# A decode attention kernel: maximum and bias moved ahead of the next keys' turns, a new order of the last loads

## The chip, the cores and the metric

The kernel runs on one core of a Trainium2 chip. The metric is the device time of one execution in microseconds (us); several executions give a median. A core has five engines that run their own instruction queues in order: TensorE (PE, matrix products), VectorE (DVE), ScalarE (ACT), GpSimd (POOL) and SyncE (SP, which here only issues loads). They wait for each other through semaphores. Sixteen DMA engines move data from the chip's memory into the core's.

## The reference

One decode step of grouped-query attention beside a token-mixing MLP, all in float32. With B = 8, D = 512, 32 query heads, 8 key/value heads, 8192 cached positions and head size 128:

```python
xn = layernorm(x)
q = xn @ wq                                   # 32 heads of 128
scores = einsum("bhqd,bhkd->bhqk", q, k) * 128 ** -0.5   # each key head serves 4 query heads
o = einsum("bhqk,bhkd->bhqd", softmax(scores), v)
out = x + o @ wo + mixer(xn)                  # mixer: layernorm, outer product with w1, + b1, gelu, product with w2
```

The key and value caches are 8 x 8 blocks of 8192 x 128 floats each: 64 blocks of keys and 64 of values, 4 MB a block, each read once.

## The kernel before, in words

The 64 pairs of a key/value head and a batch row are worked through one after the other; block i has head h = i // 8 and batch row b = i % 8. Everything is scheduled by hand: each engine executes its instructions in the order in which the program writes them, and semaphores are put in for the data and the buffers.

**Loads.** A ring of five 4 MB buffers (`raw`) holds keys and values. `load_next` (L68) takes the next entry of the list `order` and issues it on SP; each entry has a place number, 2i for the keys and 2i + 2.5 for the values of block i, and the list is sorted by it. In the kernel before, the last keys have number 124.2 (L55), so that they come right after the keys of block 62. A buffer comes free when qk (for keys) or pv (for values) has read it; `load_next` is called at the end of both. When the list is empty, the next call loads the last two heads' output weights (`wo`) into the buffer after that, as eight loads (L85). The first keys and the last values come in pieces.

**A slot.** `slot(i)` (L380) does the scores of block i, the values product of block i - 1, and prepares the keys of block i + 1:

- `qk(i)` (L222): 32 matmuls on PE from the turned keys into the scores S (tile `s`, L228).
- `turn(i, a)` (L215): DVE transposes a quarter of the keys in place, in 32 x 32 blocks (L218). qk needs all four quarters.
- `sm_max(i)` (L236): DVE takes the row maximum of S (tile `mr`, L238). `sm_bias(i)` (L241): a matmul on PE spreads the maxima (L243) and a DVE instruction takes the minimum over the head's rows as bias `nb` (L246).
- `sm_exp(i)` (L249): ACT computes exp with that bias (L252). `sm_place(i)` (L257): a permuting matmul on PE (L259) and a DVE transpose into `pt` (L261).
- `pv(i)` (L267): 32 matmuls on PE from `pt` and the values (tile `o`, L272).
- `o_pick(i)` (L281): three DVE instructions pick and add the parts that count (L283, L286, L287). `o_place(i)` (L290): a matmul puts them into the head's output (tile `mh`, L294).

After these come, in some slots, the mixer's steps on ACT and POOL, the copies of the next head's queries (`q_place`, DVE), and at a head's first slot the sums, the scaling and `o_project` for the head before (L311 to L328).

**The end.** The last two blocks are written out (L418 to L444): the order of their turns, of pv(61), pv(62) and of the picks is given there by hand; then pv(63) in four pieces as its values land, `o_last`, the scaling, one `o_project` for two heads (L320), and the output's store.

Of the kernel before, what the change touches and what calls it, by code (L numbers as in the profile page):

```python
# [14 lines left out]
B, D, HQ, HKV, SK, DH, F = 8, 512, 32, 8, 8192, 128, 1792  # L15
REP = HQ // HKV
P = 128
NT = SK // P
# [9 lines left out]
N_IT = B * HKV  # L28
# [5 lines left out]
def attn_mixer_kernel(ctx: ExitStack, tc: tile.TileContext, x, kc, vc, wq, wo, w1, b1, w2, b2, out):  # L34
# [12 lines left out]
    def misc():  # L47
        return ps_m.tile([P, 512], F32, name="misc")
# [3 lines left out]
    KR, VR = {}, {}  # L52
    order = []
    for i in range(N_IT):
        order.append((2 * min(i, N_IT - 1.9), kc, KR, i))  # L55
        order.append((2 * i + 2.5, vc, VR, i))
    order.sort(key=lambda o: o[0])
    order.reverse()
# [9 lines left out]
    def load_next():  # L68
        if order:
            _, src, to, i = order.pop()  # L70
            h, b = divmod(i, B)
            t = ring.tile([P, NT, DH], F32, name="raw")
            rows = src[b, h].rearrange("(p t) d -> p t d", p=P)
            at = 0
            for n in (NT // 4,) * 4 if to is KR and i == 0 else (NT // 2, NT // 4, NT // 8, NT // 8) if not order else (NT,):
                nc.sync.dma_start(t[:, at:at + n, :], rows[:, at:at + n, :])
                at += n
            to[i] = t
        elif HKV - 1 not in wos:
            t = ring.tile([P, NT, DH], F32, name="raw")  # L80
            t = t.rearrange("p (h r c) d -> p h r (c d)", h=4, r=REP)
            for h in (HKV - 2, HKV - 1):
                rows = wo[h * REP * DH:(h + 1) * REP * DH, :].rearrange("(r p) n -> p r n", p=P)
                wos[h] = t[:, h % 2]
                for r in range(REP):  # L85
                    nc.sync.dma_start(wos[h][:, r, :], rows[:, r, :])

    wos = {}
# [15 lines left out]
    for _ in range(RING - 2):  # L104
        load_next()
# [109 lines left out]
    def turn(i, a, w=NT // 4):  # L215
        if i < N_IT:
            t = KR[i][:, a:a + w, :].rearrange("p t d -> p (t d)")
            nc.vector.transpose(t, t)  # L218
# [3 lines left out]
    def qk(i):  # L222
        h, b = divmod(i, B)
        S[i] = ps_s.tile([P, 512], F32, name="s")
        kt = KR.pop(i).rearrange("p (u g) d -> p g u d", g=NG)
        for j in range(NB):
            for g in range(NG):
                nc.tensor.matmul(S[i][g * Q:(g + 1) * Q, :], W[h % 2][:, b, j, :], kt[:, g, :, j * Q:(j + 1) * Q],  # L228
                                 start=(j == 0), stop=(j == NB - 1))
        load_next()  # L230
# [5 lines left out]
    def sm_max(i):  # L236
        mr = work.tile([P, 1], F32, name="mr")
        nc.vector.tensor_reduce(mr, S[i], AX.X, ALU.max)  # L238
        st[i] = mr

    def sm_bias(i):  # L241
        m = misc()
        nc.tensor.matmul(m[:, :P], st[i].to_broadcast([P, P]), ident, start=True, stop=True)  # L243
        t = one.tile([P, P], F32, name="sq")
        nb = work.tile([P, 1], F32, name="nb")
        nc.vector.tensor_tensor_reduce(t, m[:, :P], hmask, -SCALE, 3.0e38, ALU.add, ALU.min, nb)  # L246
        st[i] = nb

    def sm_exp(i):  # L249
        h, b = divmod(i, B)  # L250
        p = t2k.tile([P, 512], F32, name="t2k")
        nc.scalar.activation(p, S.pop(i), AF.Exp, bias=st[i], scale=SCALE, accum_out=LR[h % 2][:, b:b + 1])  # L252
        st[i] = p
# [3 lines left out]
    def sm_place(i):  # L257
        m = misc()
        nc.tensor.matmul(m, perm, st.pop(i), start=True, stop=True)  # L259
        PT[i] = work.tile([P, 512], F32, name="pt")  # L260
        nc.vector.transpose(PT[i], m)  # L261
# [5 lines left out]
    def pv(i, u0=0, u1=NU):  # L267
        if u0 == 0:
            O[i] = ps_o.tile([P, 512], F32, name="o")
        for u in range(u0, u1):  # L270
            c = u % NB
            nc.tensor.matmul(O[i][c * Q:(c + 1) * Q, :], PT[i][:, u * Q:(u + 1) * Q],  # L272
                             VR[i][:, u * NG:(u + 1) * NG, :].rearrange("p t d -> p (t d)"),
                             start=(u < NB), stop=(u >= NU - NB))
        if u1 == NU:
            del VR[i], PT[i]
            load_next()
# [3 lines left out]
    def o_pick(i):  # L281
        om = t2k.tile([P, 512], F32, name="t2k")
        nc.vector.tensor_tensor(om.rearrange("p (g d) -> p g d", g=NG), O.pop(i).rearrange("p (g d) -> p g d", g=NG),  # L283
                                dm.unsqueeze(2).to_broadcast([P, NG, DH]), ALU.mult)
        ob = work.tile([P, 256], F32, name="ob")
        nc.vector.tensor_add(ob, om[:, :256], om[:, 256:])  # L286
        nc.vector.tensor_add(ob[:, :DH], ob[:, :DH], ob[:, DH:])  # L287
        OB[i] = ob

    def o_place(i):  # L290
        h, b = divmod(i, B)
        if b == 0:
            MH[h] = ps_h.tile([P, 512], F32, name="mh")
        nc.tensor.matmul(MH[h][:, b * REP:(b + 1) * REP], OB.pop(i)[:, :DH], sel, start=True, stop=True)  # L294
# [13 lines left out]
    def o_sums(h):  # L308
        m = misc()
        for r in range(REP):  # L310
            nc.tensor.matmul(m[:, r * B:(r + 1) * B], sel[:, r:r + 1].to_broadcast([P, P]), LR[h % 2], start=True, stop=True)  # L311
        RD[h] = work.tile([P, REP, B], F32, name="rd")
        nc.vector.reciprocal(RD[h], m[:, :REP * B].rearrange("p (r b) -> p r b", r=REP))

    def o_scale(h):
        nc.vector.tensor_tensor(OTS[h % 2].rearrange("p r (b s) -> p r b s", s=BS)[:, :, :, 0],
                                MH.pop(h)[:, :REP * B].rearrange("p (b r) -> p r b", r=REP), RD.pop(h), ALU.mult)

    def o_project(*hs):
        m = misc()  # L320
        n = 0
        for h in hs:
            for r in range(REP):
                n += 1
                for j in range(NB):
                    nc.tensor.matmul(m[j * Q:(j + 1) * Q, :D // NB], OTS[h % 2][:, r, :], wos[h][:, r, quarter[j]],  # L326
                                     start=(n == 1), stop=(n == REP * len(hs)))
        nc.vector.tensor_add(yacc, m[:, :D // NB], yacc)  # L328
# [5 lines left out]
    def mx_begin(b):  # L334
        m = misc()
        nc.tensor.matmul(m, ident[:B, b:b + 1].to_broadcast([B, P]), hn, start=True, stop=True)  # L336
        hb = one.tile([P, D], F32, name="hb")
        nc.scalar.copy(hb, m)
        acc = one.tile([P, D], F32, name="macc")
        nc.gpsimd.memset(acc, 0.0)  # L340
        mx[b] = (hb, acc)

    def mx_step(b, j):
        hb, acc = mx[b]
        g = one.tile([P, D], F32, name="g")
        nc.scalar.activation(g, hb, AF.Gelu_apprx_tanh, bias=b1t[:, j:j + 1], scale=w1t[:, j:j + 1])  # L346
        nc.gpsimd.tensor_scalar(g, g, w2t[:, j:j + 1], 1.0, op0=ALU.mult, op1=ALU.mult)  # L347
        nc.gpsimd.tensor_add(acc, acc, g)  # L348
# [25 lines left out]
    quart = NT // 4  # L374
# [3 lines left out]
    LAST = N_IT - 1  # L378

    def slot(i):  # L380

        h, b = divmod(i, B)
        qk(i)
        turn(i + 1, 0)
        sm_max(i)
        turn(i + 1, quart)
        if i:
            pv(i - 1)
        turn(i + 1, 2 * quart)
        sm_bias(i)  # L390
        if i:
            o_pick(i - 1)
            o_place(i - 1)
        sm_exp(i)
        turn(i + 1, 3 * quart)
        sm_place(i)
        if b == 0:
            mx_begin(h)
            if h:
                o_sums(h - 1)  # L400
                o_scale(h - 1)
                if h + 1 < HKV:
                    o_project(h - 1)
        k = 2 if h + 1 < HKV else 3
        for j in range(k * b, min(k * b + k, NF)):
            mx_step(h, j)
        if b == 2 and h + 2 < HKV:
            load_wo(h)
        if 3 <= b < 3 + NB and h + 1 < HKV:
            q_place(h + 1, b - 3)  # L410
        if b == (B - 1 if h + 1 < HKV else B - 3):
            mx_end(h)
# [3 lines left out]
    for i in range(LAST - 1):  # L416
        slot(i)
    h = HKV - 1  # L418
    qk(LAST - 1)
    turn(LAST, 0)  # L420
    sm_max(LAST - 1)
    turn(LAST, quart)
    sm_bias(LAST - 1)
    sm_exp(LAST - 1)
    turn(LAST, 2 * quart)
    sm_place(LAST - 1)
    turn(LAST, 3 * quart)
    qk(LAST)
    sm_max(LAST)
    sm_bias(LAST)  # L430
    sm_exp(LAST)
    pv(LAST - 2)
    o_pick(LAST - 2)
    o_place(LAST - 2)
    sm_place(LAST)
    pv(LAST - 1)
    o_pick(LAST - 1)
    o_place(LAST - 1)
    o_sums(h)
# [33 lines left out]
```

## Time and profile before

| | |
|---|---|
| median of 3 runs | 1304.92 us (1304.08 to 1305.86) |
| the profiled execution's own time | 1303.8 us |
| its span, first to last instruction | 1301.9 us |
| busy: PE, DVE, ACT, POOL | 791.1, 805.8, 289.4, 231.0 us |
| mean granted clock of TensorE | 0.765 |
| read from memory | 553.69 MB, 425 GB/s over the span |

How to read it: times are of one profiled execution. A row of the groups gives line, engine, operation, output<-inputs, shapes and count, then busy time and the mean of one in ns, then the engine's idle time just before these instructions and what ended most of it. A row in order of time gives start, duration, and for a part of the rows the idle time before in brackets. The chain of waits is followed back from the last instruction and shown in order of time: start, duration, and what it was. A row of a stretch gives its bounds and length, the busy time of PE, of PE's weight loads, of DVE, ACT and POOL with counts, then the granted clock of TensorE, the share of the DMA engines, and GB/s.

### The profile page before, as it was taken

The numbers are of one execution on the slowest core, as the hardware profiler recorded it, in microseconds if no ns is written. First come the engines' busy times: TensorE is split into PE (matmuls) and PEld (weight loads), VectorE is DVE, ScalarE is ACT, GpSimd is POOL, SyncE is SP. The second block draws the span as 40 slices with busy tenths as digits, with TensorE's granted clock in tenths as the row PEclk, the third lists the DMA queues.
The fourth block names the chain that finished last, engine by engine and source line by source line (L and its number), as shares of the span: only waits on it lengthen the run. The fifth ranks groups of instructions, "written<-read, shape, count | busy, mean of one in ns | idle before, by whom it ended". The sixth has DMA issues, their size and how long they took to land.

```text
span 1301.9 us, 12448 instructions
## 1 busy us (share of the span) xinstructions
PE 791.1 (61%) x5178; PEld 260.6 (20%) x5178; DVE 805.8 (62%) x834; ACT 289.4 (22%) x365; POOL 231.0 (18%) x244
## 2 busy tenths in 40 slices
PE   3375657755566646656558556575465775576466
PEld 2121112111121112211113111121112211122112
DVE  2676575575665665665765756755666657656662
ACT  0032221221222321212202213023121223213210
POOL 1022211212112211212112112022120222113210
PEclk9688777777778678687687786777776777767778
DMA  9999999999999999999999999999999999999995
GB/s 403 434 434 428 429 434 431 434 432 431 431 432 435 430 434 433 431 430 430 434 431 433 433 432 428 434 433 431 430 432 433 432 435 432 435 432 430 429 432 216
DMA packets 24139, 554.50 MB, mean 426 GB/s; under 512 B 2540, under 2 KB 2572, under 8 KB 6932
## 3 DMA queue, kind: packets, MB, share of 16 engines
q1 hardware_dynamic: 23940, 553.67, 98.9%
q8 instruction: 41, 0.67, 0.2%
q14 instruction: 14, 0.11, 0.0%
q0 software_dynamic: 128, 0.02, 0.0%
q10 hardware_dynamic: 16, 0.02, 0.0%
HBM read 553.69 MB, written 0.02 MB: 425 GB/s over the span
## 4 chain that ended last, share of the span: by engine, by line
DMA 58%; PE 22%; DVE 13%; issue 4%; ACT 3%; SPq 0%; ACTq 0%; DVEq 0%
DMA raw<-in_A_k_cache_dram 56%; DVE raw L218 10%; PE s L228 10%; PE o L272 6%; PE misc L259 3%; ACT L252 2%; DMA raw<-in_A_wq_dram 2%; DVE mr L238 1%; ACT t2k L252 1%; PE s L188 1%; PE misc L336 1%; PE misc L326 1%; PE misc L311 0%; DVE t2k L283 0%; DVE sq L246 0%
## 5 line engine op out<-in xcount | busy, mean ns | idle before, releaser
L218 DVE STREAM_TRANSPOSE raw<-raw 128x2048 f32<-128x2048 f32 x256 | 582.1, 2294 | 347.8 <-DMA raw<-in_A_k_cache_dram 347.8
L228 PE MATMUL s<-raw,w 128*32 128x512 f32 x2048 | 324.3, 790 | 20.3 <-issue 11.8
L347 POOL TENSOR_SCALAR g<-g,w2t 128x512 f32<-128x512 f32 x112 | 77.7, 693 | 897.5 <-ACT g L346 897.5
L272 PE MATMUL o<-raw,pt 128*32 128x512 f32 x2048 | 231.0, 592 | 0.0
L294 PE MATMUL mh<-sel,ob 128*128 128x4 f32 x126 | 35.0, 348 | 314.6 <-DVE ob L287 314.6
L252 ACT ACT_TABLE_LOAD x55 | 70.6, 1283 | 590.4 <-DVE nb L246 590.3
L348 POOL TENSOR_TENSOR macc<-macc,g 128x512 f32<-128x512 f32 x112 | 144.4, 1289 | 9.4
L259 PE MATMUL misc<-t2k,perm 128*128 128x512 f32 x128 | 125.0, 1077 | 17.2 <-ACT t2k L252 17.2
L228 PEld LDWEIGHTS s<-raw,w 128*32 128x32 f32 x2048 | 77.5, 144 | 279.5 <-issue 260.0
L346 ACT ACTIVATE g<-hb,b1t,w1t 128x512 f32<-128x512 f32 x112 | 91.0, 813 | 128.8 <-POOL macc L348 128.1
L243 PE MATMUL misc<-ident,mr 128*128 128x128 f32 x128 | 32.3, 336 | 127.7 <-DVE mr L238 127.7
L294 PEld LDWEIGHTS mh<-sel,ob 128*128 128x128 f32 x126 | 29.5, 290 | 328.6 <-DVE ob L287 328.6
L272 PEld LDWEIGHTS o<-raw,pt 128*32 128x32 f32 x2048 | 62.4, 110 | 156.9 <-issue 156.8
L252 ACT ACTIVATE t2k<-s,nb 128x512 f32<-128x512 f32 x64 | 44.0, 687 | 197.8 <-DVE nb L246 197.2
L261 DVE STREAM_TRANSPOSE pt<-misc 128x512 f32<-128x512 f32 x64 | 45.6, 712 | 39.1 <-PE misc L259 39.0
L346 ACT ACT_TABLE_LOAD x54 | 69.3, 1283 | 1.4
L238 DVE TENSOR_REDUCE mr<-s 128x1 f32<-128x512 f32 x64 | 42.2, 659 | 24.3 <-PE s L228 24.2
L243 PEld LDWEIGHTS misc<-ident,mr 128*128 128x128 f32 x128 | 19.6, 193 | 185.2 <-DVE mr L238 177.7
L283 DVE TENSOR_TENSOR t2k<-o,dm 128x512 f32<-128x512 f32 x63 | 43.2, 685 | 6.1 <-PE o L272 6.1
L211 DVE COPY w<-qt 32x128 f32<-32x128 f32 x64 | 37.0, 616 | 0.7
L259 PEld LDWEIGHTS misc<-t2k,perm 128*128 128x128 f32 x128 | 30.7, 297 | 21.6 <-ACT t2k L252 21.6
L286 DVE TENSOR_TENSOR ob<-t2k 128x256 f32<-128x256 f32 x63 | 26.8, 425 | 2.2
(75 smaller groups left out, 198.2 us busy)
## 6 DMA issues: line engine op xcount, KB each, us to landing
raw<-in_A_k_cache_dram SPq DMA_DIRECT2D x63, 4096.0 KB, 38.2
raw<-in_A_v_cache_dram SPq DMA_DIRECT2D x63, 4096.0 KB, 32.0
raw<-in_A_wq_dram SPq DMA_DIRECT2D x2, 4096.0 KB, 17.1
wo<-in_A_wo_dram SPq DMA_DIRECT2D x6, 1024.0 KB, 39.5
raw<-in_A_k_cache_dram SPq DMA_DIRECT2D x4, 1024.0 KB, 26.9
raw<-in_A_v_cache_dram SPq DMA_DIRECT2D x1, 2048.0 KB, 32.6
raw<-in_A_wo_dram SPq DMA_DIRECT2D x8, 256.0 KB, 7.3
raw<-in_A_v_cache_dram SPq DMA_DIRECT2D x1, 1024.0 KB, 34.7
```

What stands on the lines that cost most here:

```text
L218: nc.vector.transpose(t, t)
L228: nc.tensor.matmul(S[i][g * Q:(g + 1) * Q, :], W[h % 2][:, b, j, :], kt[:, g, :, j * Q:(j + 1) * Q], start=(j == 0), stop=(j == NB - 1))
L238: nc.vector.tensor_reduce(mr, S[i], AX.X, ALU.max)
L243: nc.tensor.matmul(m[:, :P], st[i].to_broadcast([P, P]), ident, start=True, stop=True)
L252: nc.scalar.activation(p, S.pop(i), AF.Exp, bias=st[i], scale=SCALE, accum_out=LR[h % 2][:, b:b + 1])
L259: nc.tensor.matmul(m, perm, st.pop(i), start=True, stop=True)
L261: nc.vector.transpose(PT[i], m)
L272: nc.tensor.matmul(O[i][c * Q:(c + 1) * Q, :], PT[i][:, u * Q:(u + 1) * Q], VR[i][:, u * NG:(u + 1) * NG, :].rearrange("p t d -> p (t d)") ...
L294: nc.tensor.matmul(MH[h][:, b * REP:(b + 1) * REP], OB.pop(i)[:, :DH], sel, start=True, stop=True)
L346: nc.scalar.activation(g, hb, AF.Gelu_apprx_tanh, bias=b1t[:, j:j + 1], scale=w1t[:, j:j + 1])
L347: nc.gpsimd.tensor_scalar(g, g, w2t[:, j:j + 1], 1.0, op0=ALU.mult, op1=ALU.mult)
L348: nc.gpsimd.tensor_add(acc, acc, g)
```

## The change

In `slot`, the maximum and the bias of block i come directly after qk(i), ahead of the first turn of the next keys; pv, pick and output placement of block i - 1 follow that first turn; then exp, the second turn, the placement of the probabilities, and the last two turns. The written-out end gets a similar order: pv(61) moves ahead of the placement of block 62, its pick behind qk(63), and pv(62) ahead of the placement of block 63. The last keys keep their regular number in the list of loads (after the values of block 61) and come in four pieces. The end weights come as one load for head 6 and two (three rows, one row) for head 7.

```diff
@@ the list of loads, load_next
-        order.append((2 * min(i, N_IT - 1.9), kc, KR, i))
+        order.append((2 * i, kc, KR, i))
...
-            for n in (NT // 4,) * 4 if to is KR and i == 0 else (NT // 2, NT // 4, NT // 8, NT // 8) if not order else (NT,):
+            for n in (NT // 4,) * 4 if to is KR and i in (0, N_IT - 1) else (NT // 2, NT // 4, NT // 8, NT // 8) if not order else (NT,):
...
-                for r in range(REP):
+                for r in (slice(0, REP),) if h < HKV - 1 else (slice(0, REP - 1), slice(REP - 1, REP)):
                     nc.sync.dma_start(wos[h][:, r, :], rows[:, r, :])
@@ slot
         qk(i)
+        sm_max(i)
+        sm_bias(i)
         turn(i + 1, 0)
-        sm_max(i)
-        turn(i + 1, quart)
         if i:
             pv(i - 1)
-        turn(i + 1, 2 * quart)
-        sm_bias(i)
-        if i:
             o_pick(i - 1)
             o_place(i - 1)
         sm_exp(i)
-        turn(i + 1, 3 * quart)
+        turn(i + 1, quart)
         sm_place(i)
+        for a in (2, 3):
+            turn(i + 1, a * quart)
@@ the end
     qk(LAST - 1)
     turn(LAST, 0)
     sm_max(LAST - 1)
-    turn(LAST, quart)
     sm_bias(LAST - 1)
     sm_exp(LAST - 1)
-    turn(LAST, 2 * quart)
+    turn(LAST, quart)
+    pv(LAST - 2)
     sm_place(LAST - 1)
-    turn(LAST, 3 * quart)
+    for a in (2, 3):
+        turn(LAST, a * quart)
     qk(LAST)
+    o_pick(LAST - 2)
+    o_place(LAST - 2)
     sm_max(LAST)
     sm_bias(LAST)
     sm_exp(LAST)
-    pv(LAST - 2)
-    o_pick(LAST - 2)
-    o_place(LAST - 2)
+    pv(LAST - 1)
     sm_place(LAST)
-    pv(LAST - 1)
     o_pick(LAST - 1)
     o_place(LAST - 1)
     o_sums(h)
```

## The prediction

> **What bounds the kernel now.** I read the page first, then one middle slot in order of time, then the chain of waits at both ends, then a table of two-microsecond stretches for the clock.
>
> ```profile
> span 1301.9 us, 12448 instructions
> PE 791.1 (61%) x5178; PEld 260.6 (20%) x5178; DVE 805.8 (62%) x834; ACT 289.4 (22%) x365; POOL 231.0 (18%) x244
> DMA  9999999999999999999999999999999999999995
> L218 DVE STREAM_TRANSPOSE raw<-raw 128x2048 f32<-128x2048 f32 x256 | 582.1, 2294 | 347.8 <-DMA raw<-in_A_k_cache_dram 347.8
> L228 PE MATMUL s<-raw,w 128*32 128x512 f32 x2048 | 324.3, 790 | 20.3 <-issue 11.8
> raw<-in_A_k_cache_dram SPq DMA_DIRECT2D x63, 4096.0 KB, 38.2
> raw<-in_A_v_cache_dram SPq DMA_DIRECT2D x63, 4096.0 KB, 32.0
> ```
>
> The DMA engines are busy in every slice but the last, and VectorE (DVE) stands idle for 347.8 us, all of it ahead of a turn and for keys that have not landed. So loading sets the pace. The lead of the loads is large: a key load is issued 38.2 us before it lands. 324.3 us over 64 blocks is 5.07 us for one qk.
>
> ```profile
> 657.24 2.31 DVE L218 STREAM_TRANSPOSE raw<-raw 128x2048 f32<-128x2048 f32 x1 [5.31 <-DMA raw<-in_A_k_cache_dram]
> 659.47 0.65 DVE L238 TENSOR_REDUCE mr<-s 128x1 f32<-128x512 f32 x1
> 660.05 4.48 DVE L218 STREAM_TRANSPOSE raw<-raw 128x2048 f32<-128x2048 f32 x2
> 664.45 0.25 DVE L246 CUSTOM_DVE_ANT_0 sq<-misc,hmask 128x128 f32<-128x128 f32 x1
> 666.03 2.30 DVE L218 STREAM_TRANSPOSE raw<-raw 128x2048 f32<-128x2048 f32 x1
> 666.92 2.08 PE L259 MATMUL misc<-t2k,perm 128*128 128x512 f32 x2 [0.17 <-ACT t2k L252]
> 669.04 0.72 DVE L261 STREAM_TRANSPOSE pt<-misc 128x512 f32<-128x512 f32 x1 [0.71 <-PE misc L259]
> 669.36 4.87 PE L228 MATMUL s<-raw,w 128*32 128x512 f32 x32
> 676.42 2.31 DVE L218 STREAM_TRANSPOSE raw<-raw 128x2048 f32<-128x2048 f32 x1 [6.48 <-DMA raw<-in_A_k_cache_dram]
> ...
> 691.70 0.36 DVE L313 RECIPROCAL rd<-misc 128x32 f32<-128x32 f32 x1 [3.09 <-PE misc L311]
> 692.40 1.94 PE L326 MATMUL misc<-wo,ot 128*32 128x128 f32 x32 [0.74 <-PE misc L311]
> ```
>
> In this slot the four turns start when the keys land at 657.24. Maximum, bias and the sums of the block before (pick) lie between the turns, on the same engine. What matters: while DVE turns, TensorE (PE) computes the values product pv of the block before, and nothing on DVE has to wait for it. Two turns from 660.05 to 664.45 cost 2.2 us each. The slot is done at 674.23, 2.2 us before the next keys land at 676.42.
>
> ```profile
> 49.19 6.08 PE s L228 x32
> ...
> 66.87 5.76 PE s L228 x32
> ...
> 121.23 2.31 DVE raw L218
> ...
> 1246.04 2.31 DVE raw L218
> ...
> 1258.39 3.84 PE s L228 x32
> ...
> 1266.23 2.09 PE misc L259 x2
> ...
> 1271.30 6.02 PE s L228 x32
> ...
> 1277.35 0.70 DVE mr L238
> ...
> 1278.10 0.49 PE misc L243 x2
> 1278.58 3.61 PE o L272 x32
> ...
> 1282.29 0.70 DVE t2k L283
> ...
> 1283.02 0.44 DVE ob L286
> ...
> 1283.48 0.30 DVE ob L287
> ...
> 1283.82 0.39 PE mh L294 x2
> 1284.21 0.96 PE misc L259 x2
> ...
> 1290.73 0.90 PE misc L311 x8
> 1291.63 3.61 PE o L272 x32
> ...
> 1296.87 1.93 PE misc L326 x64
> ```
>
> These are the chain of waits at the start (to 121.23) and at the end. The turns at 121.23 and 1246.04 are the first turns of blocks 5 and 62, each begun as its keys landed: 1124.81 us for 57 blocks, so **loading takes 19.73 us a block** (the six loads of output weights in it).
>
> **The slot's order.** No operation is added or removed in a slot; the order on DVE and PE changes, so the price is that of the waits. Before, turn(i+1, 0) needs only its keys. After, it stands behind the maximum and bias of block i, which need qk(i); and pick(i-1) stands in front of the second turn, with pv(i-1) only just issued behind the bias matmul. Queued behind that wait are three turns, the transpose of the probabilities, and then qk(i+1) on PE. The slot becomes a loop in which DVE and PE take turns. Its length from the end of qk, step by step: maximum from 1277.35, bias matmul to 1278.58, pv to 1282.20 (with pv, not the turn of 2.2 us beside it, ending last: 3.61), pick to 1283.78. With the qk before ending at 1277.32 that is 6.46. Then the second turn 2.2, the transpose 0.72 and two turns 4.4: in all 13.8 us, plus qk itself. Placement matmuls (0.39 and 0.96) fit under the second turn; exp on ScalarE is ready before them.
>
> **What qk then takes.** Rows give 3.84 (at 1258.39) to 6.08 (at 49.19). The clock is the reason:
>
> ```profile
> 1240.00:1242.00 2.00, 2.00 (x16) 0.59 (x12) 0.00 (x0) 0.81 (x1) 1.06 (x2) 0.52 1.14 492
> 1252.00:1254.00 2.00, 0.00 (x0) 0.00 (x0) 2.00 (x4) 0.39 (x1) 0.00 (x0) 0.54 0.95 410
> 1258.00:1260.00 2.00, 2.00 (x24) 0.71 (x20) 2.00 (x3) 0.00 (x0) 0.00 (x0) 0.75 0.99 426
> 1274.00:1276.00 2.00, 2.00 (x16) 0.44 (x12) 0.00 (x0) 0.00 (x0) 0.00 (x0) 0.50 0.97 408
> ```
>
> The number after the five engines is the granted clock. It falls while PE idles (0.54 from 1252) and comes back only some time into work (0.75 from 1258, in the qk of 3.84, which followed other matmuls directly). The qk of 6.02 at 1271.30 came 3.0 us after the placement matmul had ended at 1268.32 and ran at 0.50 up to 1276. In the new order the placement ends some 3 us after pv, and qk starts 9 us after pv: about 6 us without a matmul in front of every qk. The nearest rows are therefore 6.02 and 6.08, and I take 6.02. The loop is 19.8 us, just over the 19.73 that loading needs: **the compute becomes the bound**, and the wait of 347.8 us for keys disappears.
>
> The Trainium skill, page "TensorE: Matmul & The Clock Gate", section "Why this matters for your kernels", speaks against the new order too: it wants no PE gaps over about 3 us between bursts, since one idle window sends the clock back to half. By its Part 1 a qk that starts cold runs at half rate for one to two windows of 3.4 us, an estimate from that page of 5.3 to 7.0 us for qk and 19.1 to 20.8 for the loop; the rows above agree as far as they go (6.02, 6.08).
>
> **The sum.** qk(0) stays at 49.19. The first slot has no pv, and its sum in the new order (6.08, maximum and bias 1.3, bias minimum 0.4, four turns 8.8, transpose 0.72) is 17.3 against the 17.68 of the rows, so qk(1) stays at 66.9. From there 61 loops of 19.8 make 1207.8. In six slots a head ends: reciprocal, scaling and o_project, from 691.70 to 694.34 in the rows, come between the last turn and qk, 2.6 us, of which the 1.94 of matmuls give back half by raising the clock earlier: 1.6 each, 9.8 in all. qk(62) starts at 1284.5.
>
> **The end.** From the end of qk(62) at 1290.5: maximum and bias 1.27, pv(61) 3.61, placement 1.0, transpose 0.72, two turns 4.5, so qk(63) starts 11.1 later and ends at 1307.6. Then maximum and bias 1.27, pv(62) 3.61, placement 0.96, transpose 0.77, pick 1.49, its placement 0.43, the sums 0.90 (row 1290.73), the last pv 3.61, and the 6.66 from its end at 1295.24 to the end of the span: 19.7, where it was 24.6. This is the change's gain, 4.9 us, since pv(61) no longer stands behind qk(63). Against it stands qk(63) ending at 1307.6 in place of 1277.3. The end is 1327.3.
>
> **The loads.** The last keys follow V61 instead of leading it, in four pieces, and the end weights come as three loads, not eight.
>
> ```profile
> SPq L86 <- DMA raw<-in_A_v_cache_dram: 20.0, 6, 9.3
> 1288.00:1290.00 2.00, 0.74 (x8) 0.00 (x0) 1.12 (x3) 0.00 (x0) 0.00 (x0) 1.00 0.37 142
> ```
>
> SP waited 20.0 us in issuing the eight for earlier loads to land, and the last bytes came before 1290, while o_project starts at 1296.87: hidden before, hidden after. Three issues more for keys and five fewer for weights cost nothing as long as each load is issued well ahead. Between the slots the queue keeps the same order, and a load issued at the end of qk or pv has 38.2 or 32.0 us of lead. The cover goes only where loading is the bound: then V61 (half of 19.73 after K62 at 1246.04) and a quarter of the keys put the first piece at about 1258.3, the last at 1265.8, against turns that would start at about 1257 and 1271 (below): at most 1 us, beside qk(62). I take nothing, bounds 0 and 1.
>
> **The rivals.** *Loading stays the bound.* If qk keeps its mean of 5.07 us, the loop is 18.9, under 19.73, and the middle takes as long as now. For it: the mean is the mean of all 64 blocks in this kernel. Against it: there the placement matmul ran straight into qk (666.9 to 669.4 in the middle slot), and the new order puts three DVE operations between the two. Its time: K62 lands at 1246.04, four turns, pick and transpose take 11.1 (8.8, 1.49, 0.72 and the hand-overs), qk(62) starts at 1257.2 and ends at 1262.2; 11.1, 5.07 and 19.7 later the span ends at 1298.1. That is 3.8 less than now, 1301 by the median. With 6.02 for the two last blocks alone it is 1300.0, or 1303. It decides this way when 13.8 plus qk plus 0.16 (9.8 over 61) is under 19.73, so at a qk below 5.8 us.
>
> *The loop locks to the clock's steps.* The rows of the clock put its changes at 1241.92 (0.04 of a stretch of two at full clock), 1252.16 and 1259.0: 10.24 and 6.84 apart, three and two times 3.41. A qk at full clock all through is about 3.6 us (pv's 3.61 is the same 32 matmuls at 1.00), and each us at half clock adds half a us. A loop a little under 20.48, six steps, starts each qk a little earlier in its step, so that the full clock comes later and the loop grows; one over 20.48 shrinks. It would settle at 20.48, with the head's extra work swallowed by the same rule: qk(62) starts at 66.9 + 61 x 20.48 = 1316.2, takes 6.7, then 11.1, 6.7 and 19.7: 1360.4, by the median 1363. For it: the two long rows of qk (6.02, 6.08) come within 0.7 us of the 6.7 that this takes. Against it: a step that is mostly filled with qk might already bring the clock back, and then a loop near 18.8 comes in between and the mean falls to about 19.8. The Trainium skill's page named above states the ground for it in Part 1, a free-running window of 3413 ns; the steps of 3.41 in the trace agree.
>
> *The change does nothing in the middle*, because DVE's idle time covers what is added: that is the first rival seen from DVE, whose work stays 805.8 us in all. It fails because the loop counts PE's qk and pv as well.
>
> **How the numbers follow.** The sum goes by one profiled execution of 1303.8 us, 1.9 over its span; the median of the runs is 1.1 above it. 1327.3 + 1.9 + 1.1 = 1330. Chances: compute bound without locking 0.65 (1310 to 1347: 0.3 us of loop either way, times 61), locked 0.20 (1347 to 1364), loading stays the bound 0.12 (1299 to 1304), others 0.03. For 8 in 10 the range leaves out about 0.1 at each end: 1303 to 1360. Measured from no change, a difference of 0.2% (2.6 us) is about what this kernel's runs can tell. Faster by more takes the first rival with a short qk at the end: 0.08. Within 0.2%: 0.05. Slower: 0.87.
>
> **What would show it.** Right: the wait of DVE for keys (347.8 us) falls to a few tens; new waits, about 1.4 us a slot of pick for pv (3.61 less the turn of 2.2) and about 6 us a slot of qk for the last turn; the mean of qk goes from 5.07 to about 6 us; first turns come 19.8 to 20.5 us apart within a head; SP waits longer for free slots and the DMA share falls a little. From the end of qk(63) to the end of the span 19.7, not 24.6. Wrong: DVE still waiting 2 us a slot for keys, or qk with a mean under 5.8. The weakest step is the 6.02: 0.2 us on it are 12 us of the end.

## The result and the profile after

The changed kernel takes 1334.91 us (median of 4 runs, 1333.40 to 1336.38) against 1304.70 before (4 runs too): a ratio of 1.023, 95% interval 1.0213 to 1.0248. It is slower by 30.2 us; 1330 was predicted. The profiled execution has a span of 1334.5 us where that of before had 1301.9.

The page of the changed kernel: span, DMA in 40 slices, three groups (busy and mean, then the idle time before them and what ended it), and the lead of the loads in the last column.

```profile
span 1334.5 us, 12442 instructions
DMA  9999999999999999999999999999999999999991
L228 PE MATMUL s<-raw,w 128*32 128x512 f32 x2048 | 382.3, 915 | 337.1 <-issue 286.3
L218 DVE STREAM_TRANSPOSE raw<-raw 128x2048 f32<-128x2048 f32 x256 | 579.8, 2284 | 0.3 <-issue 0.2
L283 DVE TENSOR_TENSOR t2k<-o,dm 128x512 f32<-128x512 f32 x63 | 43.5, 690 | 58.4 <-PE o L272 58.4
raw<-in_A_v_cache_dram SPq DMA_DIRECT2D x63, 4096.0 KB, 15.4
raw<-in_A_k_cache_dram SPq DMA_DIRECT2D x62, 4096.0 KB, 20.2
```

The wait of the turns for keys, 347.8 us before, is 0.3 us of idle time in all. In its place pick waits 58.4 us for pv, qk sits idle before its first matmul for 337.1 us, and one qk takes 382.3 / 64 = 5.97 us, not 5.07. A key load is issued 20.2 us ahead of its landing, not 38.2: fewer loads are under way ahead of their use, and SP's waits for free buffers add up to 1194 us, not 1162. The DMA slices hardly show it; a 9 means 90% or more, and 98.9% of the engines' span on that queue has only become 97.4%.

One slot in the middle, in the chain of waits (start, duration, what):

```profile
629.87 6.64 PE s L228 x32
636.51 0.02 issue
636.53 0.70 DVE mr L238
637.24 0.04 issue
637.28 0.49 PE misc L243 x2
637.77 3.62 PE o L272 x32
641.38 0.02 issue
641.41 0.70 DVE t2k L283
...
643.35 0.98 PE misc L259 x2
644.33 5.89 issue
650.22 5.01 PE s L228 x32
...
668.93 5.89 PE s L228 x32
```

No DMA stands in it. From the end of qk to the next qk it is 13.7 us both times (636.51 to 650.22, 655.23 to 668.93), and qk itself varies: 6.64, 5.01, 5.89. The 5.89 us of "issue" are time in which DVE ends the second turn, transposes the probabilities and does the last two turns, and PE has nothing to do.

### The profile page after: what moved, and what is told of

Read it like the earlier page. It is cut to its first block, busy times and chain, and to the rows that moved or that the text cites. A ratio compares the mean times of both kernels' runs of the same rounds, so it can differ in the third digit from the quotient of the medians.

```text
span 1334.5 us, 12442 instructions
## 1 busy us (share of the span) xinstructions
PE 786.0 (59%) x5178; PEld 249.1 (19%) x5178; DVE 796.0 (60%) x834; ACT 289.4 (22%) x365; POOL 232.3 (17%) x244
## 3 DMA queue, kind: packets, MB, share of 16 engines
q1 hardware_dynamic: 24292, 553.67, 97.4%
## 4 chain that ended last, share of the span: by engine, by line
PE 57%; issue 23%; DVE 16%; DMA 2%; ACT 1%; SPq 0%; ACTq 0%; DVEq 0%
PE s L228 29%; PE o L272 17%; DVE raw L218 5%; PE misc L259 4%; DVE mr L238 3%; DVE t2k L283 3%; DVE ob L286 3%; PE misc L243 2%; DMA raw<-in_A_wq_dram 2%; PE mh L294 2%; DVE ob L287 1%; PE misc L326 1%; PE s L188 1%; ACT L346 1%; DVE pt L261 1%
## 5 line engine op out<-in xcount | busy, mean ns | idle before, releaser
L228 PE MATMUL s<-raw,w 128*32 128x512 f32 x2048 | 382.3, 915 | 337.1 <-issue 286.3
L347 POOL TENSOR_SCALAR g<-g,w2t 128x512 f32<-128x512 f32 x112 | 81.3, 726 | 908.8 <-ACT g L346 908.8
L272 PE MATMUL o<-raw,pt 128*32 128x512 f32 x2048 | 234.3, 598 | 0.0
L228 PEld LDWEIGHTS s<-raw,w 128*32 128x32 f32 x2048 | 95.1, 160 | 605.7 <-issue 545.5
L294 PE MATMUL mh<-sel,ob 128*128 128x4 f32 x126 | 24.3, 263 | 108.5 <-DVE ob L287 108.5
L283 DVE TENSOR_TENSOR t2k<-o,dm 128x512 f32<-128x512 f32 x63 | 43.5, 690 | 58.4 <-PE o L272 58.4
L259 PE MATMUL misc<-t2k,perm 128*128 128x512 f32 x128 | 72.8, 651 | 2.5 <-ACT t2k L252 2.5
L294 PEld LDWEIGHTS mh<-sel,ob 128*128 128x128 f32 x126 | 18.7, 188 | 165.6 <-DVE ob L287 164.8
L246 DVE CUSTOM_DVE_ANT_0 sq<-misc,hmask 128x128 f32<-128x128 f32 x64 | 18.6, 291 | 44.1 <-PE misc L243 44.1
L286 DVE TENSOR_TENSOR ob<-t2k 128x256 f32<-128x256 f32 x63 | 34.6, 549 | 2.1
L340 POOL MEMSET macc<- 128x512 f32 x8 | 4.2, 524 | 117.5 <-PE misc L353 117.5
## 6 DMA issues: line engine op xcount, KB each, us to landing
raw<-in_A_k_cache_dram SPq DMA_DIRECT2D x62, 4096.0 KB, 20.2
raw<-in_A_v_cache_dram SPq DMA_DIRECT2D x1, 1024.0 KB, 18.7
raw<-in_A_v_cache_dram SPq DMA_DIRECT2D x2, 512.0 KB, 20.2
```

## The experiments

The theory on record: the slot has become a loop of DVE and PE of 13.7 us plus a qk that starts at half clock, longer than the 19.73 us of loading. The rivals: the new loads cost the time; the loop is long by its waits and the clock only goes along; and, about the size, that the loop locks to the clock's steps.

### Which part

The new slot alone (old loads, old end), and everything but the new slot:

```diff
# e1_slot_only: the kernel before, with the slot of the change
# e2_end_loads: the changed kernel, with the slot of before
```

> The kernel before with the new order inside the slot alone; loads, end weights and the written-out end as before. Loop theory (the slot has become a loop through VectorE and TensorE of about 13.7 us plus a qk of about 6 us, longer than the 19.73 us that loading needs): 1335 to 1342 us, the whole loss, and some us more since the old end is kept; VectorE's wait for keys near 0. Rival (the new order of the loads, the keys in pieces or the three weight loads cost the time): about 1305 us.

> The changed kernel with the old order inside the slot; new loads, weights and end kept. Loop theory: loading is the bound again, 1300 to 1305 us, VectorE's wait for keys near 340 us. Rival (the loads cost the time): about 1335 us.

Measured: the slot alone 1337.64 us, ratio 1.0254 (1.0239 to 1.0269); without it 1304.62, ratio 0.9997 (0.9988 to 1.0007), with 350.9 us of DVE waiting for keys. The whole loss is the slot's. Two more runs take what is left apart:

```diff
# e10_loads_only: the kernel before, with the new order, pieces and weight loads
# e11_end_only: the kernel before, with the new written-out end
```

> The kernel before with the new loads alone (last keys in their regular place and in four pieces, three weight loads); slot and end as before. No theory gives them a price: 1304 to 1306 us.

> The kernel before with the new written-out end alone. The prediction's gain of 4.9 us behind qk(63) if the last pv stayed at 3.61 us: 1300 us. With the last pv at half clock as in e2_end_loads (6.43 us): 1303 to 1305 us.

Measured: 1305.07, ratio 1.0004 (0.9994 to 1.0013), and 1305.43, ratio 1.0008 (0.9998 to 1.0017). Neither is worth anything by itself, and the gain that the prediction gave to the end is missing in e2_end_loads and in e11_end_only (last pv 6.43 and 5.99 us). With the new slot the two together are worth 2.7 us: e1_slot_only, which lacks them, takes 1337.64 us and the changed kernel 1334.91.

### Is the clock a cause

Matmuls that nothing reads are added to the changed kernel, in PE's gap of the slot:

```diff
+    def warm(n):
+        m = misc()
+        for _ in range(n):
+            for g in range(NB):
+                nc.tensor.matmul(m[g * Q:(g + 1) * Q, :], bsel[:, :Q], rj.rearrange("p j i d -> p (j i d)"), start=True, stop=True)
...
         sm_place(i)
+        warm(12)        # e3_warm;  warm(6) in e5_warm_half
         for a in (2, 3):
             turn(i + 1, a * quart)
```

> The changed kernel with 48 matmuls per slot that nothing reads, set on TensorE between the placement of the probabilities and the next qk (5.2 us at full clock), while VectorE does the last two turns. No wait is removed and work is added. Loop theory with the clock as its last term: qk starts at full clock and takes 3.6 to 4.2 us, not 5.97; the loop is 17.3 to 17.9 us, under 19.73, so that loading is the bound again: 1299 to 1306 us. Rival (the loop is long by its waits and the clock only goes along with it): 1335 us or more.

Measured: 1508.86 us, ratio 1.1558 (1.1537 to 1.1579). The size was wrong: 48 such calls are 96 matmul instructions and take twice what was planned. In order of time:

```profile
675.03 10.51 PE L384 MATMUL misc<-rj,bsel 128*32 128x512 f32 x96
685.35 3.62 PE L228 MATMUL s<-raw,w 128*32 128x512 f32 x32
```

qk now waits for them, but it takes 3.62 us. So the time could not decide between the theories, and half as many were tried:

> The kernel of e3_warm with half the matmuls that nothing reads: 24 per slot, which by e3_warm take 5.25 us at full clock (48 took 10.51 there) and so fit the 5.89 us between the placement and qk. Loop theory with the clock as its last term: qk about 3.6 us as in e3_warm, loop 13.7 + 3.6 = 17.3 us, loading is the bound again: 1299 to 1306 us, though TensorE has 24 matmuls more to do in each slot. Rival (the clock only goes along with a loop that is long by its waits): 1335 us or more.

Measured: 1306.32 us, ratio 1.0013 (1.0004 to 1.0023). Its page and waits:

```profile
span 1303.7 us, 18355 instructions
L228 PE MATMUL s<-raw,w 128*32 128x512 f32 x2048 | 242.3, 615 | 35.1 <-DVE raw L218 23.3
L218 DVE STREAM_TRANSPOSE raw<-raw 128x2048 f32<-128x2048 f32 x256 | 580.2, 2286 | 87.4 <-DMA raw<-in_A_k_cache_dram 86.7
```

qk is down to 242.3 / 64 = 3.79 us, the turns wait for keys again (86.7 us), and 28.6 of the 30.2 us are gone, with no dependency removed and 24 matmul calls more in each slot. The rest of the loop is as long as before: where no keys are waited for, qk starts 17.34 us after the last one (734.59 and 751.93 in this trace), which is 13.7 and a qk of 3.64. The half clock at the start of qk is what lifts the loop over the loading time; with the gap filled the new order is 1.7 us slower than the kernel before.

### Is the wait for pv a cause

In the changed kernel, one more turn is put between pv and the pick that waits for it:

```diff
         if i:
             pv(i - 1)
+        turn(i + 1, quart)
+        if i:
             o_pick(i - 1)
             o_place(i - 1)
         sm_exp(i)
-        turn(i + 1, quart)
+        turn(i + 1, 2 * quart)
         sm_place(i)
-        for a in (2, 3):
-            turn(i + 1, a * quart)
+        turn(i + 1, 3 * quart)
```

> The changed kernel with turns between pv and what follows it: first turn, pv, second turn, pick and its placement, exp, third turn, placement of the probabilities, fourth turn. Maximum and bias stay ahead of the turns. Loop theory: VectorE no longer waits for pv (0.97 us a slot), and the loop is 1.66 + four turns 8.85 + pick 1.42 + transpose 0.65 + 0.1 = 12.7 plus a qk of 5.3 to 6.0 us: 18.0 to 18.7, under 19.73; 1300 to 1306 us, VectorE waiting about 1 us a slot for keys. Rival (maximum and bias ahead of the first turn are by themselves enough to make the compute the bound): 1320 us or more.

Measured: 1305.13 us, ratio 1.0005 (0.9995 to 1.0014). The time is as the loop theory has it: maximum and bias ahead of the turns do not cost the time by themselves. Its terms are not. DVE waits for keys only 6.5 us in all, not about 1 us a slot, and the rows say why:

```profile
583.80 1.42 POOL L348 TENSOR_TENSOR macc<-macc,g 128x512 f32<-128x512 f32 x1
584.13 1.23 DVE L287 TENSOR_TENSOR ob<-ob 128x128 f32<-128x128 f32 x1
...
590.48 6.59 PE L228 MATMUL s<-raw,w 128*32 128x512 f32 x32 [3.29 <-issue]
```

The pick's last addition, 0.30 us in the chain of before, takes 1.23 beside POOL's addition of the mixer, and ends just after it; its mean over 63 rose from 292 to 740 ns. And qk here, too, starts cold after 3.29 us of idle PE. So this loop ends close to the loading time, not 1 us under it. Over blocks 2 to 61 the mean time from the end of a qk to the next one falls only from 14.06 to 13.83 us, though the wait of 0.97 us is gone, and the mean of qk from 5.97 to 5.74 (367.3 / 64): together 0.47 us a slot, about 28 of the 29.8 us between the two kernels. The run does not give the price of the wait for pv alone, since the slower addition took most of it back.

### Does the loop lock

One and two additions on DVE that nothing reads, inside the changed kernel's loop:

```diff
+    junk = const.tile([P, 256], F32, name="junk")
+    two = rj.rearrange("p j i d -> p (j i d)")
...
         for a in (2, 3):
             turn(i + 1, a * quart)
+            if a == 2:
+                for _ in range(1):      # 2 in e6_add2
+                    nc.vector.tensor_add(junk, two[:, :256], two[:, 256:])
```

> The changed kernel with one addition on VectorE of 128 x 256 (about 0.46 us) per slot between the third and the fourth turn, inside the loop; its result is not read. Locked loop (the granted clock changes in steps of 3.41 us, and the loop settles at six of them): 20.48 us a loop, mean of qk about 6.3 us, 1355 to 1365 us. Plain loop (qk stays at 5.97): 0.46 x 62 = 28.5 us more, 1363 us. The pair with e6_add2 tells them apart.

> The same with two such additions, 0.92 us a slot. Locked loop: again 20.48 us a loop, with qk shorter than in e6_add1 (20.48 - 13.74 - 0.92 = 5.8 us), and the time within 5 us of e6_add1's. Plain loop (qk stays at 5.97): 57 us more than the changed kernel, 1392 us, and 28 us more than e6_add1.

Measured: 1361.02 (ratio 1.0434, 1.0415 to 1.0453) and 1382.32 (ratio 1.0597, 1.0578 to 1.0617), 26.1 and 47.4 us over the changed kernel. Not within 5 us of each other, so the lock as expected is refuted; the plain loop comes nearer. An addition turned out to cost less than was put down, by the rows of e6_add2 in order of time 0.375 us, half of 667.74 to 668.49:

```profile
667.74 0.83 DVE L400 TENSOR_TENSOR junk<-rj 128x256 f32<-128x256 f32 x2
668.49 2.30 DVE L218 STREAM_TRANSPOSE raw<-raw 128x2048 f32<-128x2048 f32 x1
```

At that price the plain loop gives 0.375 x 62 = 23 us for each addition, and 26.1 and 21.3 were measured. The starts of qk in the chain of waits tell more. e6_add1:

```profile
578.22 5.44 PE s L228 x32
597.71 5.92 PE s L228 x32
617.67 6.18 PE s L228 x32
637.90 6.31 PE s L228 x32
658.24 6.37 PE s L228 x32
678.66 1.89 PE s L228 x5
...
742.07 5.44 PE s L228 x32
```

and e6_add2:

```profile
587.79 6.63 PE s L228 x32
608.91 6.29 PE s L228 x32
629.71 6.14 PE s L228 x32
650.34 6.06 PE s L228 x32
670.90 6.02 PE s L228 x32
691.42 6.00 PE s L228 x32
...
755.05 6.62 PE s L228 x32
```

In e6_add1 the loops are 19.49, 19.96, 20.23, 20.34, 20.42: short of 20.48 by 0.99, 0.52, 0.25, 0.14, 0.06. In e6_add2 they are 21.12, 20.80, 20.63, 20.56, 20.52: over 20.48 by 0.64, 0.32, 0.15, 0.08, 0.04. Each loop halves the distance to six of the clock's steps, from either side: inside a head the loop does lock, as the rival had it, with a qk that lengthens or shortens until the loop fits. But the slot in which a head ends throws it off, once in eight. From one head to the next the same qk starts 163.85 us later in e6_add1 (578.22 to 742.07) and 167.26 in e6_add2 (587.79 to 755.05): 48 and 49 steps of 3.413. The changed kernel, without additions, does the same:

```profile
609.66 6.50 PE s L228 x32
...
770.12 6.49 PE s L228 x32
```

These are 160.46 us apart, and later ones, at 810.65, 971.08 and 1131.50 in its chain, 160.43 and 160.42: 47 steps. So over a head each addition costs one step, 3.41 us, where eight times 0.375 are 3.0. The totals alone cannot tell the two theories apart; the starts of qk can.

### The end

Why the end gained nothing: in e2_end_loads the last pv is not the 3.61 us of the sum. The chain at its end, and e2_end_loads with matmuls that nothing reads in the two gaps:

```profile
1274.72 5.72 PE s L228 x32
...
1285.27 1.07 PE misc L259 x2
...
1288.88 1.40 PE misc L311 x8
1290.28 6.43 PE o L272 x32
```

```diff
     sm_place(LAST - 1)
+    warm(5)
...
     sm_place(LAST)
+    warm(2)
```

> The kernel of e2_end_loads (old slot, new loads, weights and end) with 20 matmuls that nothing reads behind the placement of block 62 and 8 behind that of block 63, in TensorE's gaps of the written-out end. In e2_end_loads the last pv took 6.43 us at half clock and qk(63) 5.72, where 3.61 and 3.62 are seen at full clock. If the idle gaps ahead of them took the end's gain away: both go to about 3.6 us, 4 to 5 us less, 1299 to 1301 us, ratio 0.996 to 0.997. Rival (the end is held by the landing of the last values and weights): 1304 us as e2_end_loads.

Measured: 1299.31 us, ratio 0.9961 (0.9949 to 0.9974).

```profile
1274.22 3.68 PE s L228 x32
...
1287.24 3.62 PE o L272 x32
```

These are qk(63) and the last pv. Both are at full clock, and 5.3 us come off: the cold clock had eaten the end's gain. The same can be had by an order without gaps (several calls to a line here):

```diff
# e8_early_turns: slot and order of loads of before, weights as three loads, and this end:
     qk(LAST - 1); turn(LAST, 0); sm_max(LAST - 1); sm_bias(LAST - 1); sm_exp(LAST - 1)
+    for a in (1, 2, 3):
+        turn(LAST, a * quart)
+    pv(LAST - 2)
     qk(LAST)
+    o_pick(LAST - 2); o_place(LAST - 2); sm_max(LAST); sm_place(LAST - 1); sm_bias(LAST); sm_exp(LAST)
+    sm_place(LAST); pv(LAST - 1); o_pick(LAST - 1); o_place(LAST - 1)
# e9_early_warm: the same with warm(2) behind pv(LAST - 1)
```

> A version meant to beat both kernels. The kernel before with its slot and its order of loads; end weights as three loads; the end written anew: block 63's turns follow block 62's bias without a break, pv(61) and qk(63) follow each other on TensorE, and the placement of block 62 comes behind qk(63), that of block 63 ahead of pv(62). Worked out from rows of e2_end_loads: qk(62) ends at about 1263.6, three turns later (1270) qk(63) starts, 3.6 us at full clock, to 1274; pv(62) waits for the values of block 62 (about 1275.5), ends at 1279; pick, placement, sums 3 us, the last pv in pieces to 1286 if its clock holds or 1289 if it does not, the rest 6.7: span 1293 to 1296, time 1295 to 1298, ratio 0.993 to 0.995. Rival (the landing of the last values and weights holds the end): 1300 us or more.

> The same with 8 matmuls that nothing reads between pv(62) and the placement of its pick. If the idle time ahead of the last pv lowers its clock in e8_early_turns (last pv over 5 us), this one brings it to 3.6 us and is 1 to 3 us faster; if the last pv already takes 3.6 us there, no difference.

Measured: 1299.09, ratio 0.9961 (0.9948 to 0.9973), and 1300.24, ratio 0.9966 (0.9953 to 0.9978). Faster than both kernels, by 0.4% against the one before, but e8_early_turns is 1 us over the upper end of what was expected. The chain of e8_early_turns begins with a load:

```profile
1228.05 37.28 DMA raw<-in_A_v_cache_dram
...
1265.47 3.67 PE o L272 x32
1269.14 2.27 issue
1271.42 3.64 PE s L228 x32
...
1285.85 3.62 PE o L272 x32
```

pv(61) waits for its values until 1265.47, since the last keys are loaded ahead of them, and qk(63) starts 1.4 us later than was worked out. The last pv takes 3.62 us, so the extra matmuls of e9_early_warm had nothing to gain, as was said before it ran.

## Why the prediction was right

**The bound.** It moved from loading to the loop, as forecast; the wait for keys went from 347.8 us to nothing, and e1_slot_only has the whole loss. One sign did not come as put down: first turns 19.8 to 20.5 us apart. The loops take 18.7 to 20.4 us within a head.

**The loop.** 13.8 us without qk was predicted and 13.71 measured; qk 6.02 and 5.97. The 61 loops from qk(1) to qk(62), with the heads in them, took 1222.7 us (67.4 to 1290.1) where 1217.6 was predicted, 0.08 us a slot. The wait of pick for pv is 0.97 us in a slot, not the 1.4 that was put down: the turn that covers it starts behind the bias, later than the sum had it. Its total is 58.4 us.

**The choice of 6.02.** The prediction called it the weakest step, and it was the one that decided: by e5_warm_half the loop at a qk of 3.79 us is under the loading time. That a qk after 6 us of idle PE starts at half clock was read from rows of before, and held. That 6.02 is so near the mean is in part luck. Single qks take 4.9 to 6.6 us, and what fixes their sum is the clock's steps: over a head the loops come to 160.43 us, 47 steps, and the sum, which has no such term, gives 8 x 19.8 + 1.6 = 160.0. With 48 steps, as in e6_add1, the kernel takes 26 us more.

**The head's extra work.** Predicted 1.6 us net in six slots. The loop with a head's o_project in it is about 2.2 us longer (22.2 against 20.0), and the qk behind it takes 5.46 to 5.58 us against the mean of 5.97: net about 1.8. A term that the sum lacks comes one slot later, once a head: the pick's second addition takes 1.44 us (at 1042.66) where it took 0.42 in the slot before, beside an addition of POOL of 1.26 us (at 1042.56), and from the end of that slot's qk to the next qk it is 14.7 us, not 13.7.

**The rival of the lock.** It had a chance of 0.20 and a time of 1363. The changed kernel does not settle at 20.48: in it the loops run 19.4, 19.9, 20.2, 20.3 and then 18.7. This is the jump that was named against the rival, a step mostly filled with qk that brings the clock back. The granted clock shows where: the qk at 629.87 is at 0.50 until about 635.9 and so fills 2.6 us of one step of 3.41 and then a whole one, while the qk at 650.22 fills 2.7 us of a step and is at full clock from about 652.95. With 0.375 us of work more a slot the loop does approach 20.48 inside a head (e6_add1, 1361.02). What the prediction did not see is a lock over a whole head, and that it holds in the changed kernel too. So "compute bound without locking", its first case at 0.65, has the bound and the range right, and the "without locking" only inside a head. The Trainium skill, page "TensorE: Matmul & The Clock Gate", Part 1, gives the free-running window as 3413 ns; 160.43, 163.85 and 167.26 us, 47, 48 and 49 of them, agree.

**The end.** qk(62) started at 1290.1, 5.6 us later than predicted; from its end to qk(63) 11.08 us against 11.1. From the end of qk(63) to the end of the span it was 21.4 us, not 19.7:

```profile
1307.11 5.96 PE s L228 x32
...
1321.51 1.19 PE misc L311 x8
1322.69 4.96 PE o L272 x32
```

The terms that failed are the last pv, 4.96 us for 3.61, and the sums, 1.19 for 0.90, both for the clock: the sum took them from rows at full clock, though the new order leaves PE idle during transpose and pick just ahead of them. qk(63) ends 5.5 us later than predicted, at 1313.07; 5.5 and 1.7 make the 7.2 us by which this span is over the 1327.3 of the sum. The profiled execution was the longest of the four, 1.5 us over their median, so that the median is 4.9 us over the forecast.

**The loads.** Priced at nothing; e10_loads_only gives 1.0004 (0.9994 to 1.0013).

## What to carry to other kernels

Idle time on the engine that waits for data is the slack of the whole loop, not of that engine: moving two short steps ahead of the first data-bound step, and a wait for another engine behind it, turned two engines that overlapped into two that alternate. Before such a move, add up the loop through all engines and compare it with the loading time. And price matmuls after a gap at the clock that the gap leaves, at the end of the kernel as well as in its middle: here a few matmuls that nothing reads, or an order without the gap, were worth 5 us of 1305. Where qk's length depends on the clock, compare its starts over a whole period of the schedule: a mean that agrees can hide what sets it.

## What the runs showed of the hardware

- A loop that waits for no load, and whose qk starts at half clock, settled at whole multiples of the clock's step, here per head: 47, 48 and 49 of 3.413 us (160.43, 163.85 and 167.26). With additions in the loop, each loop inside a head halved its distance to six steps.
- An addition on DVE with both inputs in the core's memory took 1.23 us, not 0.30, beside an addition of POOL of 1.42 us that had begun before it, and ended 0.14 us after that one. The Trainium skill, page "SBUF — State Buffer", sections "Who interferes with whom" and "Summary: rules for kernel authors", describes a port pair that VectorE and GpSimd share, and a VectorE instruction with two such inputs as blocked until GpSimd's ends; the rows of e4_pick_late agree.
- One float32 matmul call of 512 columns is two matmul instructions on PE: the 48 calls of e3_warm became 96 instructions and took 10.51 us at a granted clock of 1.00.
